# One-hot compares against numbers in spare PSUM columns, the first weighing ahead of the scan, and mask rows, X rows and expert weights at other places

## The chip, the core and the metric

The kernel runs on one core of a Trainium2 chip. The core has five engines that run side by side, each through its own list of instructions in order: TensorE (PE, matrix products; its weight loads are shown as PEld), VectorE (DVE), ScalarE (ACT), GpSimd (POOL) and SyncE (SP, which here only issues transfers). Transfers (DMA) are also issued from ACT and POOL. An engine waits at an instruction until the semaphores that it names have been raised, and everything behind it on that engine waits too. SBUF is the working memory, PSUM the memory into which PE writes, in banks that the kernel names; a bank's tile here has 512 float32 columns on 128 partitions.

The metric is the time of the whole program on the device in microseconds (us).

## The reference

Two blocks in a row. The first is a recurrent cell (mLSTM) over 4 batches, 8 heads, 768 positions, head width 40:

```python
for t in range(S):
    m_new = np.maximum(f_gate[:, :, t] + m, i_gate[:, :, t])
    f_stab = np.exp(f_gate[:, :, t] + m - m_new)
    i_stab = np.exp(i_gate[:, :, t] - m_new)
    m = m_new
    C = f_stab[..., None, None] * C + i_stab[..., None, None] * np.einsum('bhd,bhe->bhde', vt, kt)
    n = f_stab[..., None] * n + i_stab[..., None] * kt
    y[:, :, t] = sigmoid(o) * (C @ q) / np.maximum(np.abs(n @ q), 1.0)
```

Its output, 3072 rows of 320, goes through the second block, a routed layer of 8 experts; a row's expert is a hash of its token number:

```python
expert_idx = token_ids * np.int64(2654435761) % np.int64(E)
for e in range(E):
    mask = expert_idx == e
    h = np.maximum(x[mask] @ w1[e], 0.0)      # 320 -> 1024
    out[mask] = h @ w2[e]                     # 1024 -> 320
```

## The kernel before

**The cell** is computed in 24 steps: step `s` is one batch (`s % 4`) and one block of 128 positions (`s // 4`), all 8 heads. Within a block the recurrence becomes products. For one step:

- PE turns k and q (`turn`, a product with the identity, L396), and a copy brings them to SBUF (`kT`, `qT`, L401, mostly on ACT);
- `scores` (L460): PE multiplies kT and qT into two PSUM banks, `sp0` and `sp1`;
- `decays` (L417 to L429): PE multiplies mask rows (`Rs`) with end rows (`L`, `Lz`) into the banks `ab`, and ACT takes the exponent into `w` (L423);
- `weigh` (L476): DVE multiplies `sp` into `w`, half by half; this frees `sp0` and `sp1` for the next step's scores;
- `apart` (L486, L488): ACT and POOL copy values into `vd`; `k_weights` (L440, `kw`) and the state's updates (`decayed` L500, L522) run on POOL;
- `state` (L512): PE's products for the next state, copied out by ACT (L516, L520); they are written into the bank in which q of step `s + 2` was turned, so they wait until that `qT` is copied;
- `attend` (L533): PE's products of `w` with the values, and of `qs` (L431) with the state, into the banks `xh0` and `xh1` in turn. They use 328 of the 512 columns;
- `divided` (L551 to L560): DVE divides and gates the result (gate: ACT, L449).

The loop over the steps is written out by hand (`for s in range(NT)`, L873), and each engine's order is the order of the code (a manual schedule). Iteration `s` turns k and q of step `s + 2`, scores and weighs step `s + 1`, and attends step `s`. Loads of k, q, v and o run through SP some steps ahead, 160 KB each.

**The gates.** The first block of positions has a short scan of its own (L789, group `g0`). A long scan over all positions (L838, 2.16 us in the profile) gives `m_sb`; from it four blocks are copied to other partitions (`m1`, L906), and group `g1` makes sums (L312 to L314), then three rows `A`, `X` and `e`, each split into bfloat16 parts (`split`, L318 and L319; `rows`, L323). `keep_a` and `keep_e` (L272, L275) store these rows in DRAM from ACT's queue, and `load_a` and `load_e` (L253, L260, L263) bring them back through SP into `Rs`, `L` and `Lz` in another layout; step 4 is the first that uses them. `Rs` also has a constant part, the mask, in its last 64 partitions, written for batch 0 and copied to batches 1 to 3 (L837, L856).

**The routing** runs in pieces between the steps (`pieces`, `products`). In steps 8 to 19 `route_hot` (L717) compares a slot's column and row with the numbers 0 to 127 (`iota_f`, float32 in SBUF): `oh_c` (L720, 94 elements) and `oh_r` (L728, 256 elements), both on DVE; ACT and POOL scale `oh_c` (L724, L725). PE adds them up to a table of indices every third step (L736).

**The passage into the experts.** After the last step the rows `x` are stored to DRAM, gathered by expert through POOL (`gather`, L111; `fetch`, L1188), stored by slot (`x_slots`), and loaded in blocks of 32 (`blocks`, L1205, twelve transfers `xb`), which DVE turns (L1215). Expert 0 takes another way: its rows are turned by PE, the last 32 of them in `turn_rest` (L1220) by way of a tile `remT`. PE fills the time with expert 0's first two tiles. The weights of expert 1 are asked for (`load_weights(1)`, L1235) ahead of the first gathers. Experts 1 to 7 follow one after another, each layer by seven half products in place of eight (L1065, L1073, L1149).

Of the kernel before, what the change touches and what calls it, by code (L numbers as in the profile page):

```python
# [9 lines left out]
F32 = mybir.dt.float32  # L10
# [5 lines left out]
ALU = mybir.AluOpType  # L16
PSUM = bass.MemoryType.PSUM

P = 128
NEG = -1e30  # L20
# [3 lines left out]
def kernel(  # L24
# [24 lines left out]
    nc = tc.nc  # L49
# [145 lines left out]
    with tc.tile_pool(name="gates", bufs=1) as gp, \  # L195
# [202 lines left out]
        def turned_out(s, what, copy=nc.scalar.copy):  # L398
            d = st[s]
            d[what + "T"] = wk.tile([P, PR, P], F32, name=what + "T", bufs=3)  # L400
            copy(d[what + "T"][:], d["tp"][:])  # L401
# [313 lines left out]
        oh_c = gp.tile([P, TH, 3, NC], BF16, name="oh_c")  # L715

        def route_hot(i):  # L717
            half = TH // 3
            ts, th = slice(i * half, (i + 1) * half), slice(i % 3 * half, (i % 3 + 1) * half)
            nc.vector.tensor_tensor(  # L720
                oh_c[:, th, 0], iota_f[:, :NC].unsqueeze(1).to_broadcast([P, half, NC]),
                rc[:, 1, ts].unsqueeze(2).to_broadcast([P, half, NC]), op=ALU.is_equal,
            )
            nc.scalar.activation(oh_c[:, th, 1], oh_c[:, th, 0], AF.Copy, scale=pcol[:, 0:1])  # L724
            nc.gpsimd.tensor_tensor(  # L725
                oh_c[:, th, 2], oh_c[:, th, 0], thi[:, ts].unsqueeze(2).to_broadcast([P, half, NC]), op=ALU.mult,
            )
            nc.vector.tensor_tensor(  # L728
                oh_r[:, th], iota_f[:].unsqueeze(1).to_broadcast([P, half, P]),
                rc[:, 0, ts].unsqueeze(2).to_broadcast([P, half, P]), op=ALU.is_equal,  # L730
            )
# [65 lines left out]
        direct_a(2, nc.sync)  # L797
        nc.gpsimd.memset(Ls[0][:32].rearrange("p b t -> p (b t)").bitcast(F32), 0.0)
        ends_rows(Ls[0])
        load(2, "q")  # L800
# [15 lines left out]
        load(3, "v")  # L816
        load(5, "q")
        g0.ends()
        g0.split("e")
        g0.rows("e", nc.scalar.copy)  # L820
        turned_out(0, "k")
        turned_in(0, "q", "tr")
        turned_out(0, "q", nc.vector.tensor_copy)
        turned_in(1, "k", 0)
        kt = st[1].pop("tp")
# [10 lines left out]
        g0.weights(kwT0)  # L836
        nc.vector.tensor_copy(Rs[HB:, 1], R[HB:])  # L837
        nc.vector.tensor_tensor_scan(m_sb[:, 1:], f_sb[:], i_sb[:], NEG, op0=ALU.add, op1=ALU.max)  # L838
        st[1]["tp"] = kt
        turned_out(1, "k")  # L840
        st[1]["tp"] = qt
        turned_out(1, "q")
        pads(ks[2], qs[2])
        for t in vs[:2]:
            nc.gpsimd.memset(t[:, :, D:], 2.0)
        nc.gpsimd.memset(vds[0][:], 0.0)
        k_weights(0)
# [7 lines left out]
        weigh(0)  # L855
        nc.vector.tensor_copy(Rs[HB:, 2:B], R[HB:].unsqueeze(1).to_broadcast([P - HB, B - 2, H, P]))  # L856

# [15 lines left out]
        for s in range(NT):  # L873
# [20 lines left out]
            if s == 1:  # L894
                g1.rows("e", nc.scalar.copy)
                keep_e(0, g1.zt, nc.scalar)
                load(KV, "k")
            if s == 7:
                nc.scalar.activation(g2.t["X"][:, 0], g2.t["A"][:, 0], AF.Exp)
# [4 lines left out]
            if s == 0:  # L904
                for j in range(NB - 2):
                    nc.scalar.copy(m1[j * BH : (j + 1) * BH], m_sb[:, (j + 1) * P : (j + 2) * P + 1])  # L906
                g1.sums(False)
                g1.split("A")
            if s == 3:
                g1.weights(kwT1)  # L910
            if s + 1 < NT:
                k_weights(s + 1)
            if s == 0:
                nc.gpsimd.memset(vds[1][:], 0.0)
                for t in vs[2:]:
                    nc.gpsimd.memset(t[:, :, D:], 2.0)
                pads(ks[4], qs[4])
            if s + 1 < B:
                nc.gpsimd.memset(Cs[s + 1][1][:], 0.0)
            if s == 1:  # L920
                pads(ks[5], qs[5])
                ends_rows(Ls[1])
                nc.gpsimd.tensor_copy(Lx[:], one[:, 1].to_broadcast([P, HB]))
                load_e(1)
                load(KV - 2, "v")
                load(KV, "q")
                load(KV - 2, "o")
            for piece in pieces.get(s, []):
# [3 lines left out]
            if s + 1 < NT:  # L932
                scores(s + 1)
                decays(s + 1)
            state(s)
            if s == 0:
                nc.scalar.activation(g1.t["X"][:, 0], g1.t["A"][:, 0], AF.Exp)
                g1.rows("A", nc.scalar.copy)
# [8 lines left out]
            gate(s)  # L947
            if s == 0:
                g1.rows("X", nc.scalar.copy)
                keep_a(0, g1.zt, nc.scalar)  # L950
                load_a(B, 2 * B)
                load(3, "o")
            if s == 2:
# [45 lines left out]

    def turn(xg, dst, on_act):  # L1000

# [5 lines left out]
        if on_act:  # L1007
            nc.scalar.copy(dst, tp[:])
        else:
            nc.vector.tensor_copy(dst, tp[:])  # L1010

# [171 lines left out]
    with tc.manual_schedule():  # L1183
# [36 lines left out]
        def turn_rest():  # L1220
            remT = xp.tile([P, DB, P], F32, name="remT", bufs=1)
            turn(xr0, remT[:], True)
            nc.gpsimd.tensor_copy(xT0[:, :, NM:], remT[:, :, :RM])

# [9 lines left out]

        load_weights(1)  # L1235
        fetch(0)
        fetch(1)
        blocks(1)
        h = h0
# [89 lines left out]
```

## Time and profile before

| | us |
|---|---|
| median of 3 runs | 355.13 (354.95 to 355.22) |
| the profiled execution's own time | 349.56 |
| its span, first to last instruction | 347.7 |
| PE busy in it | 330.7 (95%) |
| DVE busy | 234.6 (67%) |
| POOL busy | 208.5 (60%) |
| ACT busy | 131.9 (38%) |

All times of single instructions below come from the one profiled execution. A line of a timeline reads: start, length, engine, line of the code, operation, tile written and tiles read, sizes, count, and in brackets how long the engine had been idle before and what released it. "x2" on a line means that two instructions in a row were put together. A matmul's end is modelled, so a busy PE is not PE at its peak. The chain of work that ended last is followed back from the last instruction, at each step to what released it. In a wait's line stand who waited, for whom, the total in us, how often, and the longest.

### The profile page before, as it was taken

The page shows a single profiled execution, that of the slowest core. Times are in us where ns is not written, and L with a number is a line of the kernel's source. Part 1 is how long each engine was busy: PE and PEld are TensorE (multiplying, and loading weights), DVE is VectorE, ACT ScalarE, POOL GpSimd, SP SyncE. Part 2 cuts the span into 40 slices and gives each one's busy share as a digit, 9 for nine tenths or more (in the row PEclk, how much of TensorE's full clock was granted, in tenths as well). Part 3 has the DMA queues.
Part 4 walks back from the last instruction along what each step waited for, and adds up shares of the span by engine and source line. Part 5 has one row for each costly group of instructions (what it writes and reads, how often), then busy time and mean ns, then how long its engine had stood idle before and what let it go on. Part 6 is the DMA issues. An engine that isn't in the chain of part 4 may idle for free.

```text
span 347.7 us, 10265 instructions
## 1 busy us (share of the span) xinstructions
PE 330.7 (95%) x4059; PEld 292.5 (84%) x4059; DVE 234.6 (67%) x526; ACT 131.9 (38%) x343; POOL 208.5 (60%) x324
## 2 busy tenths in 40 slices
PE   8879997899999899899999999999999999999994
PEld 8668987898999676578899899879989889899892
DVE  6986999999998771137676696734685775764710
ACT  4757666677777431021511411411421501511510
POOL 7783786798885314624925956933954946627613
PEclk9978999999999999999999999999999999999998
DMA  6879898999799989666959658677378478001001
GB/s 127 170 144 183 146 185 150 184 191 201 155 203 261 248 290 309 194 131 149 326 140 272 221 98 266 209 177 254 119 162 277 116 169 251 2 18 41 1 20 41
DMA packets 161960, 59.12 MB, mean 170 GB/s; under 512 B 140372, under 2 KB 157392, under 8 KB 161880
## 3 DMA queue, kind: packets, MB, share of 16 engines
q1 hardware_dynamic: 156678, 47.47, 58.4%
q0 software_dynamic: 3168, 10.49, 9.0%
q10 hardware_dynamic: 2064, 0.48, 0.6%
q8 instruction: 33, 0.54, 0.6%
q14 instruction: 17, 0.14, 0.1%
HBM read 46.25 MB, written 12.33 MB: 168 GB/s over the span
## 4 chain that ended last, share of the span: by engine, by line
PE 75%; DVE 12%; POOL 4%; issue 3%; DMA 3%; ACT 1%; another core or an unknown queue 1%; POOLq 0%; DVEq 0%
PE mh L1065 20%; PE mh L1149 15%; PE mh L1116 10%; PE mh L1073 6%; PE xh L533 6%; PE tr L396 5%; PE sp L460 4%; DVE w L476 2%; DVE oh_c L720 2%; DMA x_rows<-x 1%; PE mh L159 1%; DVE qs L431 1%; POOL xg L111 1%; PE mh L1229 1%; PE ab L419 1%
## 5 line engine op out<-in xcount | busy, mean ns | idle before, releaser
L991 POOL DMA_INDIRECT out_dram<-zo,s_idx x26 | 26.7, 1027 | 67.7 <-issue 41.1
L1116 PE MATMUL mh<-w2t,h 128*128 128x320 f32 x160 | 45.1, 433 | 0.5 <-DVE h L166 0.5
L1116 PEld LDWEIGHTS mh<-w2t,h 128*128 128x128 f32 x160 | 30.0, 190 | 11.8 <-DVE h L166 1.0
L1051 DVE TENSOR_TENSOR h<-u,mh 128x416 f32<-128x416 f32 (+1 forms) x56 | 25.4, 476 | 16.5 <-PE mh L1073 8.6
L111 POOL DMA_INDIRECT xg<-x_rows,g_idx x24 | 23.5, 977 | 15.0 <-issue 6.4
L1065 PE MATMUL mh<-tx,sw 128*128 128x208 f32 x168 | 31.9, 339 | 0.0
L1065 PEld LDWEIGHTS mh<-tx,sw 128*128 128x128 f32 x168 | 29.7, 190 | 0.1
L1051 DVE TENSOR_TENSOR u<-m,mh 128x416 f32<-128x416 f32 x28 | 16.5, 588 | 18.8 <-PE mh L1065 14.9
L1149 PE MATMUL mh<-tw,sh 128*128 128x160 f32 x168 | 27.4, 299 | 0.0
L533 PE MATMUL xh<-v,w 128*64 128x41 f32 x384 | 26.7, 231 | 0.0
L460 PE MATMUL sp<-qT,kT 64*64 64x64 f32 (+1 forms) x960 | 24.5, 238 | 2.3 <-DVE w L476 2.0
L460 PEld LDWEIGHTS sp<-qT,kT 64*64 64x64 f32 x960 | 20.5, 137 | 7.2 <-issue 3.7
L476 DVE TENSOR_TENSOR w<-sp,w 128x384 f32<-128x384 f32 x48 | 24.3, 546 | 2.4 <-ACT w L423 2.3
L533 PEld LDWEIGHTS xh<-v,w 128*64 128x64 f32 x384 | 25.2, 141 | 0.0
L1149 PEld LDWEIGHTS mh<-tw,sh 128*128 128x128 f32 x168 | 24.3, 190 | 0.0
L423 ACT ACTIVATE w<-ab 128x384 f32<-128x384 f32 x48 | 21.0, 482 | 7.5 <-PE ab L422 4.8
L1065 PE MATMUL mh<-xT,w1t 128*128 128x208 f32 x112 | 23.1, 339 | 0.0
L522 POOL TENSOR_TENSOR C<-C,add 40x164 f32<-40x164 f32 x32 | 16.2, 505 | 9.2 <-ACT dec L495 6.8
L1073 PE MATMUL mh<-xT,w1c 64*128 64x208 f32 x224 | 21.6, 342 | 0.0
L1079 ACT COPY m<-mh 128x416 f32<-128x416 f32 x14 | 7.1, 506 | 37.2 <-PE mh L1065 34.2
L1149 PE MATMUL mh<-w2t,h 128*128 128x160 f32 x112 | 21.0, 300 | 0.0
L987 ACT COPY zo<-mh 128x320 f32<-128x320 f32 x12 | 5.1, 427 | 41.9 <-PE mh L1116 26.7
(276 smaller groups left out, 859.7 us busy)
## 6 DMA issues: line engine op xcount, KB each, us to landing
w2t<-in_moe_w_dram SPq DMA_DIRECT2D x7, 1280.0 KB
w1t<-in_moe_w_dram SPq DMA_DIRECT2D x7, 1024.0 KB
xb<-x_slots SPq DMA_DIRECT2D x84, 52.0 KB
k<-in_k_dram SPq DMA_DIRECT2D x24, 160.0 KB
v<-in_v_dram SPq DMA_DIRECT2D x24, 160.0 KB
og<-in_o_gate_dram SPq DMA_DIRECT2D x24, 160.0 KB
q<-in_q_dram SPq DMA_DIRECT2D x23, 160.0 KB
x_slots<-xg SPq DMA_DIRECT2D x7, 480.0 KB
```

Source lines behind the costliest of these rows:

```text
L111: nc.gpsimd.indirect_dma_start(out=xg, out_offset=None, in_=x_d[:rows, :], in_offset=bass.IndirectOffsetOnAxis(ap=idx, axis=0),)
L396: nc.tensor.transpose(tp[:, j, :], d[what][:, 2 * j : 2 * j + 2, :].rearrange("p h d -> p (h d)"), ident[:])
L423: nc.scalar.activation(w[:, hf], ab, AF.Exp)
L460: nc.tensor.matmul(sp[hf][o * HB : (o + 1) * HB, m, bs], lhsT=kT[r, 2 * m + j, i], rhs=qT[r, 2 * m + j, ts], start=True, stop=True,)
L476: nc.vector.tensor_tensor(d["w"][:, hf], d["sp"][hf], d["w"][:, hf], op=ALU.mult)
L533: nc.tensor.matmul(xh[half[i], hs], lhsT=lhsT, rhs=rhs, start=first[i], stop=last, skip_group_check=True)
L991: ins = nc.gpsimd.indirect_dma_start(out=out[:, :], out_offset=bass.IndirectOffsetOnAxis(ap=idx, axis=0), in_=zo[:], in_offset=None, bound ...
L1051: nc.vector.tensor_tensor(o, a, b, op=ALU.add)
L1065: nc.tensor.matmul(pair(bank[n])[:, a], lhsT=lhsT(g + a), rhs=rhs, start=first and a == 0, stop=True, skip_group_check=True,)
L1073: nc.tensor.matmul(pair(bank[n])[:, a], lhsT=w1c[k, g + a, :], rhs=xT[k, 2, r], start=False, stop=True, skip_group_check=True,)
L1116: nc.tensor.matmul(zp, lhsT=h[:, fb, j * P : (j + 1) * P], rhs=w[2][:, fb, :], start=(fb == 0), stop=(fb == FB - 1),)
L1149: nc.tensor.matmul(bank[n], lhsT=lhsT(f), rhs=rhs(f), start=first and f == 0, stop=f == FB // 2 - 1, skip_group_check=True,)
```

## The change

- **Compares.** Two ACT copies, in iterations 4 and 5, write `iota_f` into columns 384 to 511 of the banks `xh1` and `xh0`, which `attend` leaves unused. `route_hot` reads the numbers from there; in each iteration it takes the bank that `divided` has just read, not the one that PE is writing.
- **Start.** The first weighing comes ahead of the long scan on DVE. The mask copies L837 and L856 become one, ahead of most of the start's DVE work. Two of the four copies to `m1` go from ACT to POOL, and they and the sums of `g1` come after step 1's `kw`. Some POOL memsets come earlier.
- **Rows.** Making and storing the rows `X` and `e` of `g1` goes from iterations 0 and 1 to behind the state products of iteration 1. The loads of these rows, and of q 6 and o 4, come behind the gate of iteration 1; o 3 is asked for before the loop, k 6 and v 4 ahead of the rows.
- **Passage.** `turn_rest` copies 32 columns straight to `xT0`, by ACT, without `remT` and POOL. `load_weights(1)` comes after the first two fetches.

```diff
+        numbers = [t[:, 3 * P :] for t in xhs]
+
         def route_hot(i):
             half = TH // 3
+            iota = numbers[(i + 1) % 2]
...
-                oh_c[:, th, 0], iota_f[:, :NC].unsqueeze(1).to_broadcast([P, half, NC]),
+                oh_c[:, th, 0], iota[:, :NC].unsqueeze(1).to_broadcast([P, half, NC]),
...
-                oh_r[:, th], iota_f[:].unsqueeze(1).to_broadcast([P, half, P]),
+                oh_r[:, th], iota[:].unsqueeze(1).to_broadcast([P, half, P]),
...
         nc.gpsimd.memset(Ls[0][:32].rearrange("p b t -> p (b t)").bitcast(F32), 0.0)
+        pads(ks[2], qs[2])
+        for t in vs[:2]:
+            nc.gpsimd.memset(t[:, :, D:], 2.0)
+        nc.gpsimd.memset(vds[0][:], 0.0)
         ends_rows(Ls[0])
...
         load(5, "q")
+        load(3, "o")
...
         turned_out(0, "q", nc.vector.tensor_copy)
+        nc.vector.tensor_copy(Rs[HB:, 1:B], R[HB:].unsqueeze(1).to_broadcast([P - HB, B - 1, H, P]))
...
         g0.weights(kwT0)
-        nc.vector.tensor_copy(Rs[HB:, 1], R[HB:])
-        nc.vector.tensor_tensor_scan(m_sb[:, 1:], f_sb[:], i_sb[:], NEG, op0=ALU.add, op1=ALU.max)
...
-        pads(ks[2], qs[2])
-        for t in vs[:2]:
-            nc.gpsimd.memset(t[:, :, D:], 2.0)
-        nc.gpsimd.memset(vds[0][:], 0.0)
...
         weigh(0)
-        nc.vector.tensor_copy(Rs[HB:, 2:B], R[HB:].unsqueeze(1).to_broadcast([P - HB, B - 2, H, P]))
+        nc.vector.tensor_tensor_scan(m_sb[:, 1:], f_sb[:], i_sb[:], NEG, op0=ALU.add, op1=ALU.max)
...
             if s == 1:
-                g1.rows("e", nc.scalar.copy)
-                keep_e(0, g1.zt, nc.scalar)
                 load(KV, "k")
+                load(KV - 2, "v")
...
             if s == 0:
-                for j in range(NB - 2):
+                for j in range(2):
                     nc.scalar.copy(m1[j * BH : (j + 1) * BH], m_sb[:, (j + 1) * P : (j + 2) * P + 1])
-                g1.sums(False)
-                g1.split("A")
...
                 k_weights(s + 1)
             if s == 0:
+                for j in range(2, NB - 2):
+                    nc.gpsimd.tensor_copy(m1[j * BH : (j + 1) * BH], m_sb[:, (j + 1) * P : (j + 2) * P + 1])
+                g1.sums(False)
+                g1.split("A")
...
-                load_e(1)
-                load(KV - 2, "v")
-                load(KV, "q")
-                load(KV - 2, "o")
...
             state(s)
+            if s == 1:
+                g1.rows("X", nc.scalar.copy)
+                keep_a(0, g1.zt, nc.scalar)
+                g1.rows("e", nc.scalar.copy)
+                keep_e(0, g1.zt, nc.scalar)
...
             gate(s)
-            if s == 0:
-                g1.rows("X", nc.scalar.copy)
-                keep_a(0, g1.zt, nc.scalar)
+            if s in (4, 5):
+                nc.scalar.copy(numbers[(s - 1) % 2], iota_f[:])
+            if s == 1:
                 load_a(B, 2 * B)
-                load(3, "o")
+                load_e(1)
+                load(KV, "q")
+                load(KV - 2, "o")
...
-    def turn(xg, dst, on_act):
+    def turn(xg, dst, on_act, n=P):
...
-            nc.scalar.copy(dst, tp[:])
+            nc.scalar.copy(dst, tp[:, :, :n])
...
-            remT = xp.tile([P, DB, P], F32, name="remT", bufs=1)
-            turn(xr0, remT[:], True)
-            nc.gpsimd.tensor_copy(xT0[:, :, NM:], remT[:, :, :RM])
+            turn(xr0, xT0[:, :, NM:], True, RM)
...
-        load_weights(1)
         fetch(0)
         fetch(1)
+        load_weights(1)
         blocks(1)
```

More of the change, by code (lines that the diff above doesn't have):

```diff
@@ L1007, in turn @@
         if on_act:
-            nc.scalar.copy(dst, tp[:])
+            nc.scalar.copy(dst, tp[:, :, :n])
         else:
-            nc.vector.tensor_copy(dst, tp[:])
+            nc.vector.tensor_copy(dst, tp[:, :, :n])
     def bank(i):
```

## The prediction

> **What bounds the kernel now.** I read the page first, then the chain of work that ended last in order of time, then single engines' timelines at the places where the chain leaves PE. Columns of the chain: start, length, engine, tile, line.
>
> ```profile
> span 347.7 us, 10265 instructions
> PE 75%; DVE 12%; POOL 4%; issue 3%; DMA 3%; ACT 1%; another core or an unknown queue 1%; POOLq 0%; DVEq 0%
> ```
>
> ```profile
> 9.91 0.42 DVE Rs L837
> 10.36 2.16 DVE m_sb L838
> 12.53 0.91 DVE w L476 x2
> 13.47 2.30 DVE Rs L856
> ...
> 22.88 1.93 PE xh L533 x21
> 24.81 1.90 PE tr L396 x8
> 26.71 1.43 PE sp L460 x32
> ...
> 33.85 0.93 PE xh L533 x21
> 35.06 0.87 PE tr L396 x8
> 35.93 0.86 PE sp L460 x32
> ...
> 55.87 1.79 DVE oh_c L720
> ...
> 60.06 0.51 DVE xh L559
> ...
> 61.16 1.73 DVE oh_c L720
> ...
> 65.29 0.51 DVE xh L559
> ...
> 70.11 0.86 PE sp L460 x32
> ...
> 74.46 0.86 PE sp L460 x32
> ...
> 79.98 1.00 DVE oh_c L720
> ```
>
> Three quarters of the chain are PE, and those the change leaves alone. It touches three places where PE is held: the start (10 to 33 us), steps 8 to 10 and 13 (55 to 82 us), and the passage into the experts (126 to 160 us). I call the gains there A, B and C.
>
> **A, the start.**
>
> ```profile
> 10.19 1.00 ACT L423 ACTIVATE w<-ab 128x384 f32<-128x384 f32 x2 [0.27 <-PE ab L422]
> 12.73 1.23 ACT L906 COPY m<-m_sb 32x129 f32<-32x129 f32 x4
> ...
> 19.70 0.41 ACT L323 COPY zt<-X_zt 128x256 bf16<-128x256 bf16 x1 [1.59 <-DVE X_zt L318]
> ...
> 20.56 0.59 ACT L401 COPY kT<-tr 128x512 f32<-128x512 f32 x1 [0.46 <-PE ab L422]
> ...
> 21.52 0.42 ACT L323 COPY zt<-e_zt 128x256 bf16<-128x256 bf16 x1
> ...
> 22.41 0.33 ACT L486 COPY vd<-v 64x164 f32<-64x164 f32 x1 [0.47 <-POOL L L376]
> ```
>
> ```profile
> 21.73 0.78 PE L512 MATMUL tr<-v,kw 128*40 128x41 f32 x16 [1.28 <-issue]
> ```
>
> ```profile
> DVE L L835 <- ACT L L834: 1.9, 1, 1.9
> ```
>
> *DVE.* Today the first weighing starts at 12.53, behind the scan (2.16), though the first half of its exponent was ready at about 10.7 (10.19 and half of 1.00). Behind it stands the mask copy (2.30), and the gate sums start at its end, 15.8. In the new order weighing runs 10.7 to 11.7, the scan to 13.9. Of the four copies of the scan's result (1.23/4 = 0.31 each) two go to POOL, beside the other two; so the sums start at about 14.7, 1.1 earlier. The mask copy goes to the DVE idle of 1.9 ahead of L835: at 0.42 for a third of it, about 1.3, hidden; without that cover it would cost up to 2.3. The POOL memsets that move ahead only exchange places with POOL work that is not yet waited for; POOL's two copies cost at most 0.6 there.
>
> *ACT.* ACT is free at 18.1 (19.70 less the wait of 1.59), but the kT copy starts at 20.56: 2.45 us go to waiting for X, its rows and the issue of their store. From 21.52 to 22.41 another 0.9 goes to the e rows and their store. Both leave, so the vd copy that releases PE's values at 22.88 could end 3.3 earlier. Next late is then PE itself: the decays of step 2 end at 20.45 (21.73 less 1.28 idle), 1.1 earlier by the DVE, 19.35; after half a us of state products the values start at about 19.9 instead of 22.9: **3.0**.
>
> *Clock.*
>
> ```profile
> 22.00:24.00 2.00, 1.63 (x34) 1.51 (x30) 1.54 (x4) 1.56 (x5) 1.71 (x5) 0.50 0.24 66
> ```
>
> In this row (PE, PEld, DVE, ACT, POOL busy, granted clock, DMA share, GB/s) PE ran at half clock. The three blocks from 22.88 took 1.93 + 1.90 + 1.43 = 5.26, the same blocks later 0.93 + 0.87 + 0.86 = 2.66. Without the stall ahead of them I expect full clock: **2.6**. It could be nothing (a rival below).
>
> The fall came behind idle stretches of 1.28 at most. The Trainium skill, "TensorE: Matmul & The Clock Gate", Part 1, has the clock halved after an idle window of about 3.4 us. By that rule a busier PE cannot be gated here and the 2.6 is safe; but by it the clock should not have fallen before either, so the trace disagrees, and I leave room for a gate that also falls in the new order.
>
> *What is paid.* The X and e rows with both stores (about 1.7 of ACT) now stand in step 1, ahead of its gate and of step 2's kT and qT copies, for which PE's state products wait. That costs between 0 and 1.7; I take 0.6, since ACT waits for PE's transposes there. Second, the mask and end rows come back through DRAM later:
>
> ```profile
> SPq L244 <- DMA gate_rows<-zt: 4.7, 1, 4.7
> ```
>
> ```profile
> 27.96 0.36 SPq L263 DMA_DIRECT2D Lz<-gate_ends  x1
> ```
>
> ```profile
> 32.81 0.30 PE L419 MATMUL ab<-Rs,Lz 128*64 128x256 bf16 x1
> ```
>
> Today the store goes out at 20.1, the last load back (Lz) at 27.96, 7.8 later, and step 4's decays use it at 32.81. In the new order the store goes out at about 20.9 (state products copied out at 20.4, X rows 0.4). With the same 7.8, Lz goes out at 28.7, and PE wants it at 32.81 - 5.0 = 27.8; the landing comes on top (below the 4.9 from 27.96 to 32.81). So the bounds are 0 and 5. Against that, SP's 4.7 of waiting for that store falls on fewer loads: o of step 3, k of 6 and v of 4 now go ahead of the rows. I take 0.5, near the lower end. **A = 3.0 + 2.6 - 0.6 - 0.5 = 4.5**.
>
> **B, the compares.**
>
> ```profile
> L720 DVE TENSOR_TENSOR oh_c<-iota_f,rc x12: 364/1050/1874, 55.8 to 106.8; 128x94 bf16<-128x94 f32 x12
> ```
>
> ```profile
> 62.05 0.71 POOL L440 TENSOR_TENSOR kw<-k,kwT 128x320 f32<-128x320 f32 x1
> ```
>
> The same compare of 94 elements takes 0.36 to 1.87 (ns: least, median, most), so most of it is waiting. It ends at 62.9 in step 9 and POOL's kw ends at 62.76: it waits until POOL's row of operations is over. DVE sets the step there, 60.06 to 65.29 = 5.23, against 70.11 to 74.46 = 4.35 where PE sets it. With 0.36 the DVE's step is 5.23 - 1.73 + 0.36 = 3.9, so PE's 4.35 is next: 0.88 in each of the two steps with 1.79 and 1.73, and about 0.4 each in the next step and in that of 79.98 (PE has the table products there). **B = 2.5**, from 0 to 3.
>
> The Trainium skill, "SBUF — State Buffer", section "Who interferes with whom", says that a VectorE instruction with two SBUF inputs contends with a GpSimd one that reads SBUF, and one with a single SBUF input does not. By it the wait is gone and B stands; without it B is 0. No compare with a PSUM operand is in this trace.
>
> The two copies of the numbers into the banks (steps 4 and 5) are 128 elements on ACT, some 0.3 each by the vd copy (0.33 for 164), beside PE; uncovered 0.6.
>
> **C, the passage into the experts.**
>
> ```profile
> 138.94 2.42 PE L1116 MATMUL mh<-w2t,h 128*128 128x320 f32 x8 [0.46 <-DVE h L166]
> ...
> 148.48 1.35 PE L159 MATMUL mh<-xT,w1t 128*128 128x160 f32 x8 [2.15 <-POOL xT L1223]
> ```
>
> ```profile
> 147.62 0.48 ACT L1008 COPY remT<-mh 128x384 f32<-128x384 f32 x1 [5.75 <-PE mh L1116]
> ```
>
> ```profile
> 145.40 0.37 SPq L1196 DMA_DIRECT2D x_slots<-xg  x1
> ```
>
> ```profile
> 157.44 1.47 DVE L1215 STREAM_TRANSPOSE xT<-xb 128x1248 f32<-128x1248 f32 x1
> ```
>
> ```profile
> 132.00:134.00 2.00, 2.00 (x13) 1.52 (x13) 0.00 (x0) 0.04 (x1) 0.00 (x0) 1.00 1.09 355
> ...
> 144.00:146.00 2.00, 2.00 (x11) 1.38 (x9) 0.00 (x0) 0.00 (x0) 1.59 (x2) 1.00 0.60 169
> ```
>
> PE waits 2.15 for the last 32 columns of xT. Today ACT copies 384 columns (147.62) and POOL 96 of them on; the new code copies the 96 at once: PE can start at about 147.9 instead of 148.48, 0.6. Why ACT starts only at 147.62 no row tells; if that goes too, another 1.5. The 0.46 ahead of 138.94 is DVE held by the gather; the gather comes sooner when expert 1's weights no longer load beside the last x store: 0.46. Sum 1.1 to 2.6; I take **C = 1.5**, near the lower end.
>
> What is paid: the weights now go out behind the x_slots store at 145.40. They are 2 x 320 x 1024 x 4 B = 2.62 MB: 7.4 us at 355 GB/s, so they land at 153.2, and expert 1's twelve xb loads queue behind. DVE wants those at 157.44, less what C gains. At 355 GB/s that fits.
>
> **The sum.** 4.5 + 2.5 + 1.5 = 8.5 off the profiled execution's 349.56 (span 347.7 and 1.86 around it): 341.1. The shown runs have a median of 355.13, 5.57 above the profiled one; I carry that over: 355.13 - 8.5 = **346.6**.
>
> **The rivals.**
> - *The start stays cold, or the rows come late.* Short idle stretches still halve the clock, or PE waits at step 4 for Lz: A = 4.5 - 2.6 = 1.9, total 5.9, 349.2. For: the clock fell behind 1.28 of idle; 7.8 us of round trip. Against: PE has less idle in the new order.
> - *The compares still wait* (the change does not do what it says): rc is still read from SBUF beside POOL. B = 0, 349.1. Against: the weighing, with one operand in PSUM, takes 0.91 for two halves (12.53) with POOL at work beside it.
> - *Expert 1's weights come late.* If they share the DMA engines with gathers and stores, xb lands some 4 later than wanted: C = -2.5, total 4.5, 350.6.
> - *Slower.* The same queue at its worst: the weights get only the 169 GB/s of 144 to 146 us (15.5, until 161.3) and the twelve xb loads follow one after another, 4.4 more at the 0.37 that SP needs for an issue: 165.7, 8.3 later than 157.44. Then PE waits 8.3, A and B give 7: 1.3 slower, 356.4. It decides from a landing at 164.4 (below some 185 GB/s). Against: most gathers are over by then.
>
> **How the numbers follow.** Forecast 0.57, cold start or late rows 0.20, compares 0.07, weights late 0.10, slower 0.04, all given back (no change) 0.02. Lower end: A 5.0, B 3.0, C 2.6, 344.5, with 0.5 for the spread of runs 344.0. Upper end: the third rival and 1.2 for parts of two rivals together, 351.8. About 0.2% is what a measurement of this kernel can tell from no change. Faster 0.94, within 0.2% 0.02, slower 0.04.
>
> **What would show it.** Right: first weighing near 10.7; step 1's values near 20 at full clock; no oh_c compare over 0.5; steps 9 to 11 at 4.4 to 4.6; no PE idle ahead of L159. Wrong: a granted clock of 0.5 at 20 to 28 us; PE waiting for ab at step 4; compares still ending with POOL's kw; PE idle at the first products of expert 1 on xb or weights.

## The result, and the profile after

| | before | after |
|---|---|---|
| median of the runs taken side by side | 354.2 us | 357.46 us |
| the profiled execution | 349.56 us (span 347.7) | 357.73 us (span 355.8) |

The changed kernel takes 1.0119 times as long, with a 95% interval of 1.0072 to 1.0167: **1.2% slower**, where 346.6 us and a gain had been forecast. The ratio and its interval are taken from the faster runs of each kernel, those within 1.5% of its fastest, while the medians are of all twenty.

Read stage by stage, the two traces tell where the time went. Their sizes need care: the profiled execution of the kernel before is a quick one, 4.6 us under its median, that of the changed kernel 0.3 over its own. So of the 8.2 between the two some 4 are the change's (1.2%), and the rest is the spread between executions, to which the last experiments come back. First the page of the changed kernel, its span and the shares of the chain that ended last:

```profile
span 355.8 us, 10265 instructions
...
PE 63%; DMA 9%; DVE 8%; POOL 6%; issue 5%; SPq 5%; ACT 2%; POOLq 0%; DVEq 0%; ACTq 0%
```

PE held 75% of the chain before. Now it holds 63%; DMA has gone from 3 to 9, and SP's queue (SPq), which was not there, has 5. So the chain has left the engine that the change relieved. The three places in order:

**The start came true in its order, though not in its size.** DVE's timeline, then PE's, of the changed kernel (start, length, engine, line, operation, out<-in; in brackets the idle time ahead of it and what ended it):

```profile
10.05 1.07 DVE L476 TENSOR_TENSOR w<-sp,w 128x384 f32<-128x384 f32 x2 [0.55 <-ACT w L423]
...
14.29 0.29 DVE L312 TENSOR_TENSOR a_zt<-f,m 128x128 f32<-128x128 f32 x1 [1.51 <-POOL m L915]
```

```profile
19.58 0.26 PE L533 MATMUL xh<-vd,w 128*64 128x82 f32 x1
...
29.73 0.30 PE L419 MATMUL ab<-Rs,Lz 128*64 128x256 bf16 x1 [1.26 <-DMA Lz<-gate_ends]
...
46.26 0.93 PE L460 MATMUL sp<-qT,kT 64*64 64x128 f32 x40
...
51.68 0.93 PE L460 MATMUL sp<-qT,kT 64*64 64x128 f32 x40
...
56.04 0.93 PE L460 MATMUL sp<-qT,kT 64*64 64x128 f32 x40
...
82.65 0.93 PE L460 MATMUL sp<-qT,kT 64*64 64x128 f32 x40
```

The weighing starts at 10.05, the gate sums at 14.29, step 1's values at 19.58 (before: 12.53, 15.8, 22.88). PE does wait for the late Lz row, 1.26.

**The compares came true.** From the scores at 51.68 on, the steps last 4.36. The answer on the tile oh_c (least, median, most, in ns) has no waiting compare left:

```profile
L723 DVE TENSOR_TENSOR oh_c<-xh,rc x12: 247/248/249, 52.6 to 102.5; 128x94 bf16<-128x94 f32 x12
```

The same marks in PE's timeline of the kernel before:

```profile
49.36 0.93 PE L460 MATMUL sp<-qT,kT 64*64 64x128 f32 x40
...
88.25 0.93 PE L460 MATMUL sp<-qT,kT 64*64 64x128 f32 x40
```

So the changed kernel is 3.1 ahead at the scores of step 8, where the compares begin (46.26 against 49.36), and 5.6 ahead at the scores of step 16 (82.65 against 88.25). That lead is then lost, and more than the lead, in two places.

**First loss: the tail of the attention.** The chain of waits of the changed kernel in order of time (start, length, what), only its DMA pieces:

```profile
89.52 3.62 DMA gate_ends<-zt
...
94.42 4.33 DMA v<-in_v_dram
...
106.57 5.81 DMA v<-in_v_dram
...
119.02 6.05 DMA xg<-x_rows,g_idx
```

In the kernel before this stretch of the chain is PE nearly throughout, from 83.96 to 109.70. Now it hangs on transfers: the store of the gate ends, two loads of v, and the gather of expert 0's rows. Four marks show where the lead goes. They are lines of SP's, PE's, POOL's and DVE's timelines, first of the changed kernel:

```profile
89.52 0.44 SPq L275 DMA_DIRECT2D gate_ends<-zt  x1
...
114.03 1.38 PE L460 MATMUL sp<-qT,kT 64*64 64x128 f32 x40
...
117.66 1.06 POOL L111 DMA_INDIRECT xg<-x_rows,g_idx  x1 [9.36 <-DVE qs L431]
...
125.09 0.20 DVE L970 COPY xg<-xg 128x64 f32<-128x64 f32 x1 [2.67 <-DMA xg<-x_rows,g_idx]
```

and of the kernel before (where DVE's copy does not wait):

```profile
89.37 0.38 SPq L275 DMA_DIRECT2D gate_ends<-zt  x1
...
120.21 1.39 PE L460 MATMUL sp<-qT,kT 64*64 64x128 f32 x40
...
115.54 1.06 POOL L111 DMA_INDIRECT xg<-x_rows,g_idx  x1 [2.88 <-DVE den L552]
```

PE is 5.6 ahead at step 16, but SP, which issues the loads one behind the other, stands at the same place at the same time (89.52 and 89.37). So its second store of the first ten steps' results goes out no earlier either (108.41, before 107.53), and the gather, which needs those rows, goes out 2.1 later. The wait for a v load costs PE 1.3 of its lead at step 20; at the scores of step 23, its last, it is still 6.2 ahead (114.03 against 120.21). Nearly all is lost behind that: POOL stands 9.36 at the gather, with the copy of `vd` for which PE waits behind it in its list, and DVE waits for the gathered rows. The table by stretches of ten us shows what PE does meanwhile (PE, PEld, DVE, ACT, POOL busy, granted clock, DMA share, GB/s):

```profile
110.00:120.00 10.00, 6.31 (x160) 5.39 (x160) 7.61 (x20) 4.73 (x14) 2.04 (x3) 0.94 0.90 237
120.00:130.00 10.00, 7.61 (x75) 6.61 (x76) 2.93 (x14) 1.33 (x3) 2.23 (x5) 0.55 0.82 275
```

It idles in part from 110 on, and from 120 its clock is down to 0.55. The lead has become a lag of 2.3 at the first product of expert 0 (L159: 128.97, before 126.64, both below).

**Second loss: the passage.** PE's timeline of the changed kernel, then of the kernel before:

```profile
128.97 1.99 PE L159 MATMUL mh<-xT,w1t 128*128 128x256 f32 x8
...
163.34 1.76 PE L1072 MATMUL mh<-xT,w1t 128*128 128x208 f32 x4 [4.86 <-DVE xT L1222]
165.91 4.36 PE L1072 MATMUL mh<-tx,sw 128*128 128x208 f32 x12 [0.81 <-DVE tx L1034]
```

```profile
126.64 1.99 PE L159 MATMUL mh<-xT,w1t 128*128 128x256 f32 x8
...
159.12 0.87 PE L1065 MATMUL mh<-xT,w1t 128*128 128x208 f32 x4
159.82 2.34 PE L1065 MATMUL mh<-tx,sw 128*128 128x208 f32 x12
```

Expert 1's products start 4.2 later, wait within their first group, and run at a lowered clock (0.66 granted from 160 to 170 us): the group of 12 takes 4.36 in place of 2.34. They wait for DVE's transpose, DVE for xb, and xb for SP. SP's timeline, changed kernel first, kernel before second:

```profile
143.35 0.37 SPq L1203 DMA_DIRECT2D x_slots<-xg  x1
143.82 0.43 SPq L98 DMA_DIRECT2D w1t<-in_moe_w_dram  x1
...
147.25 12.61 SPq L1218 DMA_DIRECT2D xb<-x_slots  x12
```

```profile
148.67 6.08 SPq L1211 DMA_DIRECT2D xb<-x_slots  x12
```

The x_slots store is 2.05 earlier than before (145.40), yet the twelve loads behind the weights take 12.61 to issue where they took 6.08, and end 5.1 later. All that follows is shifted by this wait and the lowered clock: 8.1 at the end of the span (355.8 less 347.7).

### The profile page after: what moved, and what is told of

It reads as the page before. It is cut to its first block, busy times and chain, and to the rows that moved or that the text cites. A ratio compares the mean times of both kernels' runs of the same rounds, so it can differ in the third digit from the quotient of the medians.

```text
span 355.8 us, 10265 instructions
## 1 busy us (share of the span) xinstructions
PE 331.9 (93%) x4059; PEld 293.9 (83%) x4059; DVE 229.4 (64%) x525; ACT 131.7 (37%) x343; POOL 206.5 (58%) x325
## 4 chain that ended last, share of the span: by engine, by line
PE 63%; DMA 9%; DVE 8%; POOL 6%; issue 5%; SPq 5%; ACT 2%; POOLq 0%; DVEq 0%; ACTq 0%
PE mh L1072 20%; PE mh L1156 15%; PE mh L1123 8%; PE mh L1080 6%; PE xh L533 3%; SPq L1218 3%; PE tr L396 3%; DMA xg<-x_rows,g_idx 3%; DMA v<-in_v_dram 3%; PE sp L460 2%; DVE w L476 2%; PE mh L1234 1%; DVE qs L431 1%; DMA gate_ends<-zt 1%; PE ab L419 1%
## 5 line engine op out<-in xcount | busy, mean ns | idle before, releaser
L1072 PE MATMUL mh<-tx,sw 128*128 128x208 f32 x168 | 33.9, 354 | 0.8 <-DVE tx L1034 0.8
L1072 PEld LDWEIGHTS mh<-tx,sw 128*128 128x128 f32 x168 | 31.5, 200 | 1.5 <-DVE tx L1034 1.4
L1072 PE MATMUL mh<-xT,w1t 128*128 128x208 f32 x112 | 24.0, 348 | 4.9 <-DVE xT L1222 4.9
L533 PE MATMUL xh<-v,w 128*64 128x41 f32 x384 | 27.5, 235 | 0.0
L533 PEld LDWEIGHTS xh<-v,w 128*64 128x64 f32 x384 | 26.1, 145 | 0.0
L1072 PEld LDWEIGHTS mh<-xT,w1t 128*128 128x128 f32 x112 | 20.3, 195 | 5.4 <-DVE xT L1222 5.4
L533 PE MATMUL xh<-vd,w 128*64 128x82 f32 x192 | 20.8, 251 | 3.7 <-issue 3.7
L460 PE MATMUL sp<-qT,kT 64*64 64x64 f32 (+1 forms) x960 | 23.6, 233 | 0.5 <-DVE w L476 0.3
```

The lines of the kernel that those rows point to most:

```text
L460: nc.tensor.matmul(sp[hf][o * HB : (o + 1) * HB, m, bs], lhsT=kT[r, 2 * m + j, i], rhs=qT[r, 2 * m + j, ts], start=True, stop=True,)
L533: nc.tensor.matmul(xh[half[i], hs], lhsT=lhsT, rhs=rhs, start=first[i], stop=last, skip_group_check=True)
L1072: nc.tensor.matmul(pair(bank[n])[:, a], lhsT=lhsT(g + a), rhs=rhs, start=first and a == 0, stop=True, skip_group_check=True,)
```

## The experiments

Two theories had to be told from their rivals. **P** (the passage): the weights of expert 1, put ahead of xb on SP's queue, cost 4 to 6 us. **S** (supply): the tail of the attention is set by the row loads, and what start and compares gain is waited away there. For S spoke rows that the prediction had not looked at, the same table by stretches for the kernel before:

```profile
60.00:70.00 10.00, 9.13 (x236) 8.19 (x234) 9.49 (x22) 6.93 (x21) 7.25 (x16) 1.00 1.00 180
70.00:80.00 10.00, 10.00 (x279) 9.14 (x280) 9.45 (x24) 7.42 (x21) 9.15 (x18) 1.00 1.02 199
80.00:90.00 10.00, 9.52 (x258) 8.60 (x254) 9.50 (x24) 6.69 (x19) 8.88 (x18) 1.00 1.07 206
```

The last but one number is the DMA share: the engines were already full from 60 to 90 us, at some 200 GB/s. Ratios are to the kernel before in runs on the same chip; that kernel's median differed between the groups of runs (351.8 to 355.3), so only ratios are compared across groups.

### Each part alone

**The weights put back ahead, in the changed kernel:**

```diff
+        load_weights(1)
         fetch(0)
         fetch(1)
-        load_weights(1)
```

> The changed kernel with one thing put back: the weights of expert 1 are loaded ahead of the first fetches again, as in the kernel before. Theory P (the passage: behind the fetches the weights' 2.62 MB stand ahead of expert 1's twelve xb loads on the same queue, and xb lands about 4 us late): 4 to 6 us less than the changed kernel, ratio to the kernel before 0.995 to 1.001, and DVE's transpose of xb starts within 3 of the end of the attention plus 30, as before, with no idle PE at the first products of expert 1. Rival (the loss comes from the attention alone, and the weights only fill time that was lost already): ratio stays near 1.012.

Measured: 0.9991 (0.9956 to 1.0026). The changed kernel's 1.0119 less this is 1.3%, 4.5 us. PE's wait at expert 1 fell from 4.86 to 1.39, in PE's timeline of this run:

```profile
162.10 0.97 PE L1072 MATMUL mh<-xT,w1t 128*128 128x208 f32 x4 [1.39 <-DVE xT L1222]
```

P holds, though not all idle time went. It also says that the rest of the change, for which some 8 of the 8.5 us had been forecast, brings nothing that can be measured (1.6 us at most by the interval).

**The same move alone, in the kernel before:**

```diff
-        load_weights(1)
         fetch(0)
         fetch(1)
+        load_weights(1)
```

> The kernel before with that one move alone: the weights of expert 1 behind the two fetches. Theory P: 4 to 6 us slower, ratio 1.011 to 1.017, with PE idle 3 or more at the first products of expert 1. Rival (the prediction's sum: the weights fit, and the gather comes 0.46 sooner): ratio 0.998 to 1.001.

Measured: 1.0193 (1.0146 to 1.0241), 6.8 us slower, a little over what P gave. SP's and PE's timelines show the same two marks:

```profile
148.73 14.29 SPq L1211 DMA_DIRECT2D xb<-x_slots  x12
```

```profile
166.82 1.76 PE L1065 MATMUL mh<-xT,w1t 128*128 128x208 f32 x4 [5.54 <-DVE xT L1215]
```

**The compares alone, in the kernel before** (weights, start and rest rows as before):

```diff
+            iota = numbers[(i + 1) % 2]
...
-                oh_c[:, th, 0], iota_f[:, :NC]...
+                oh_c[:, th, 0], iota[:, :NC]...
...
+            if s in (4, 5):
+                nc.scalar.copy(numbers[(s - 1) % 2], iota_f[:])
```

> The kernel before with the compares' numbers in the output banks alone. The prediction's B: 2.5 us less, ratio 0.993. Theory S (the tail of the attention is set by the row loads, whose DMA engines are busy 0.87 to 1.07 of the time from 30 to 120 us, so what PE gains in steps 8 to 13 is waited away later): the steps 9 to 11 shrink to 4.3 to 4.6 and scores of step 14 start 2 earlier, but step 23 starts at most 0.7 earlier and the ratio is 0.997 to 1.001. Third theory (the copies into the banks or the new reads cost): ratio above 1.002.

Measured: 1.0016 (0.9984 to 1.0049): nothing. Yet the compares themselves do all that was forecast, as the tile's row shows:

```profile
L723 DVE TENSOR_TENSOR oh_c<-xh,rc x12: 248/250/250, 54.9 to 104.8; 128x94 bf16<-128x94 f32 x12
```

At the end of the attention DVE's copies of the gathered rows wait, here 2.76 and then 2.55 more (DVE's timeline), and the gather itself only goes out at 119.87 (POOL's):

```profile
124.35 0.20 DVE L968 COPY xg<-xg 128x64 f32<-128x64 f32 x1 [2.76 <-DMA xg<-x_rows,g_idx]
```

```profile
119.87 1.06 POOL L111 DMA_INDIRECT xg<-x_rows,g_idx  x1 [9.33 <-DVE qs L431]
```

**The start alone, in the kernel before** (all hunks of the change but those of the compares, the weights and the rest rows):

> The kernel before with the start of the changed kernel alone (first weighing ahead of the scan, mask rows and X rows at their new places); compares, expert 1's weights and the copy of the rest rows as before. The prediction's A: 4.5 us less, ratio 0.987. Theory S: step 8 starts some 3 earlier, but the end of the attention is at most 1 earlier, ratio 0.997 to 1.002. Third theory (the new order harms the tail by itself): ratio above 1.004.

Measured: 0.9967 (0.9941 to 0.9993), 1.2 us faster, a quarter of the 4.5. S's limit of 1 us was about right.

### Is it the loads?

Fewer packets, the same bytes, read from other rows of DRAM, once in the kernel before and once in e1:

```diff
-                eng.dma_start(og[s][:], rows_of(o_gate, s))
+                eng.dma_start(og[s].rearrange("p h d -> p (h d)"), moe_w2[s % 8, :P, :])
```

> The kernel before, with the 24 loads of o reading whole rows of the second weights (128 packets of 1280 B) in place of o's rows (640 packets of 256 B): the same bytes, a fifth of the packets; o's values are left out of the result. Theory S (the DMA engines, busy with 256 B packets, set the tail of the attention; PE sets it only up to step 16): DMA share of 60 to 110 us falls from about 1.0 to about 0.8, SP's last v load goes out 4 or more earlier, and since PE of the kernel before was hardly later than the loads, the gain is 1 to 4 us: ratio 0.989 to 0.997. Rival (PE and its helpers set the tail): DMA share falls, ratio 0.998 to 1.002.

> The changed kernel with expert 1's weights ahead of the fetches again, and the same wide loads of o (o's values left out of the result). Theory S: with the loads out of the way the gains of the start and of the compares reach the end of the attention: no wait for v over 1, the gather of the first expert rows goes out 4 or more earlier than in e1, and it beats the run with wide loads of o in the kernel before by 4 to 6 us (ratio to the kernel before 0.972 to 0.984). Rival G (not the loads but the landing of the gather alone holds the tail): v waits go, but the time is that of e1 (ratio 0.996 to 1.002).

Measured: 0.9843 (0.9791 to 0.9895) for e5 and 0.9725 (0.9669 to 0.9780) for e6, medians 348.27 and 343.23 of the same group of runs. With the loads relieved, start, compares and rest rows together bring 5.0 us; with the loads as they are they brought nothing (e1). That is S's main prediction, and the rival that only the gather's landing counts falls as it was put, though the gather came earlier too. e5 gained a little more than expected: its last v load goes out at 102.22 in place of 110.60, though its DMA share did not fall evenly (0.82, 1.01 and 0.69 in the three stretches from 60 to 90 us). In e6 the gather goes out at 108.58, 9.6 ahead of e1. The first products of expert 0 in e5, then of expert 0 and expert 1 in e6, with no wait for the transpose (PE's timelines):

```profile
123.08 1.99 PE L159 MATMUL mh<-xT,w1t 128*128 128x256 f32 x8
```

```profile
119.81 1.99 PE L159 MATMUL mh<-xT,w1t 128*128 128x256 f32 x8
...
152.13 0.87 PE L1072 MATMUL mh<-xT,w1t 128*128 128x208 f32 x4
```

**Packets or bytes?** In e1, o's loads cut to the first half of each row:

```diff
-                eng.dma_start(og[s][:], rows_of(o_gate, s))
+                w = D if s < 6 else D // 2
+                eng.dma_start(og[s][:, :, :w], rows_of(o_gate, s)[:, :, :w])
```

(o's six buffers are fixed tiles here, so that the half not loaded holds an earlier step's values.)

> e1 with the loads of o from step 6 on reading the first half of each row only (640 packets of 128 B in place of 256 B; the second half of o's values is left from an earlier step, so the result leaves them out). If packets set the pace of the row loads: no gain on e1, ratio 0.996 to 1.003. If bytes set it: an eighth of the row loads' bytes less, and most of the gain of e6: ratio 0.975 to 0.988.

Measured: a median of 351.2 with runs from 341.38 to 355.27, beside 355.26 for the kernel before; the runs spread too far for an interval. Inconclusive in time. In the one trace of it the scores keep their pace of 4.35 to 4.7 up to step 22, where e1 lost 1.6 at step 20, so there half the bytes relieved the loads too, which speaks against packets alone; the gather still went out at 114.54 and DVE waited 4.9 for it. What the pace depends on, packets, bytes or SP's place for a next transfer, stays open.

### Where in the tail?

**The early transposes of the gathered rows behind the last step, in e1:**

```diff
-            if s == NT - 2:
-                for j in range(2):
-                    nc.vector.tensor_copy(xg0[:, j, Dm:], xg0[:, j, 2 * P : Dm])
-                early_turn(0)
...
         store(NT - 1, nc.gpsimd)
+        for j in range(2):
+            nc.vector.tensor_copy(xg0[:, j, Dm:], xg0[:, j, 2 * P : Dm])
+            early_turn(j)
```

(and `early_turn(1)` of step 23 likewise)

> e1 with the copies and transposes of the gathered rows (which stand ahead of DVE's division of step 22 and of PE's work of step 23) behind the last step. Loads and stores as in e1. If the wait for the gather only holds DVE and PE in order (rival G): the division of step 22 starts near 119.5 in place of 126.9, that of step 23 near 122.5 in place of 130.4, the first products of expert 0 start about 2.5 earlier, ratio 0.990 to 0.995. If the attention's own loads hold it: ratio as e1, 0.997 to 1.002.

Measured: 0.9996 (0.9962 to 1.0030). A miss: the divisions did move ahead (step 22 at 121.44 in place of 126.89, step 23 at 123.06 in place of 130.43), and expert 0's first products with them (126.55 in place of 130.32), but the second gather then took 6.31 where it took 3.65 in the kernel before, and expert 1's products start at 163.15, no earlier than in e1 (162.10). Freeing DVE and PE alone moves the wait on.

**SP's two stores of the first ten steps' results five steps ahead, in e1:**

```diff
-            if s in (18, 19):
-                store_first((s - 18) * LS // 2, (s - 17) * LS // 2)
+            if s in (13, 14):
+                store_first((s - 13) * LS // 2, (s - 12) * LS // 2)
```

> e1 with SP's two stores of the first ten steps' results in steps 13 and 14 in place of 18 and 19: the same transfers, at a place where the row loads still have a lead of some 10 us. Theory S with the gather as its last link (the gather waits for the second store, which waits in SP's queue behind row loads): the gather goes out near 110 in place of 118, DVE does not wait for it, the attention ends 4 to 7 earlier than in e1, ratio 0.980 to 0.990. Rival (the DMA engines have no room anywhere: the same bytes only move, and rows of k and v are now late): waits for k or v grow by 3 or more, ratio 0.997 to 1.005.

Measured: 0.9872 (0.9819 to 0.9924). The gather goes out 6.7 earlier than in e1, at 111.50 (POOL's timeline of e8, below), and expert 0's first products start at 123.34 in place of 130.32. That the gather now waits 0.61 and no longer 9.69 shows that it was the store that it had waited for, whatever engine its row names. The row loads are later for it, as the rival had it, but by less than the 3 that it named: the scores of step 20 come 7.2 after those of step 19, in e1 5.9. The chain has one wait for v:

```profile
111.50 1.06 POOL L111 DMA_INDIRECT xg<-x_rows,g_idx  x1 [0.61 <-DVE ta L760]
```

```profile
96.07 3.73 DMA v<-in_v_dram
```

So both S and its rival have a part: a transfer at a better place frees the gather, but the row loads pay for it.

### Do the gains pass when the transfers stand better?

Four kernels with the stores of e8 and the last row loads a step later; with neither part, with both, with the start, with the compares (the last three with the rest rows copied at once):

```diff
-            if s == B * (NB - 2):
-                fetch_rows(s + B)
+            if s == B * (NB - 2) + 1:
+                fetch_rows(s + B - 1)
```

> The kernel before with its transfers moved only: SP's two stores of the first ten steps' results in steps 13 and 14 in place of 18 and 19, and the loads of the last four steps' rows from DRAM one step later than their store in place of right behind it (SP stood 3.6 for that store's landing in e1). Theory S: the gather goes out near 111, nothing waits for it; PE sets the rest, so a few us at most: ratio 0.985 to 0.996. Rival (in the kernel before PE alone sets the tail): 0.998 to 1.002.

> The changed kernel with expert 1's weights ahead of the fetches and the same two moves of transfers, so e8 with the row loads a step later. Theory S: the wait of 3.7 for a v load after it shrinks to under 2, step 20 starts near 100.5 in place of 102.6, the first products of expert 0 near 121 in place of 123.3: ratio 0.975 to 0.985, and 4 to 6 us less than e9 (the gains of start and compares pass). Rival D (the DMA engines themselves, busy 1.0 from 60 to 120 us, hold the tail wherever the transfers stand): the wait only moves to another load; ratio as e8, 0.985 to 0.990, and under 2 us less than e9.

> e10 with the compares as in the kernel before (their numbers in SBUF): the start alone, with relief. Theory S: some 2 slower than e10, 3 to 4 faster than e9. Rival D: within 1 us of e10.

> e9 with the compares on numbers in the output banks (and the rest rows copied at once, as in e10): the compares alone, with relief. Theory S: about 2 faster than e9, 3 slower than e10. Rival D: within 1 us of both.

| kernel | median | ratio to before |
|---|---|---|
| e9, the kernel before with relief | 349.97 | 0.9882 (0.9806 to 0.9958) |
| e10, start and compares | 348.18 | 0.9849 (0.9785 to 0.9913) |
| e11, start | 346.43 | 0.9776 (0.9706 to 0.9845) |
| e12, compares | 348.19 | 0.9883 (0.9816 to 0.9951) |

The relief alone is worth 1.2%. On top of it the two parts together bring 1.8 us by the medians, not 4 to 6, and the intervals overlap. But in the one trace of e9 there was little to pass on: PE ran its start at full clock and its first compares hardly waited (both below), so the scores of step 16 start at 84.19, only 1.5 behind e10's 82.74. In e11 and e12 they start at 85.00 and 84.86. Expert 0's first products start at 124.95, 125.38, 123.23 and 124.82 in e9 to e12: whoever led at step 16 does not lead there. That is what rival D says, that the row loads hold the tail wherever the other transfers stand; how much of a larger lead would pass, these four runs do not show. Nor did e10's marks come: expert 0's first products start at 125.38, not near 121, and its chain has two waits for v in place of e8's one:

```profile
88.71 5.31 DMA v<-in_v_dram
...
95.77 5.18 DMA v<-in_v_dram
```

e11 is the fastest of the four, 2.2% under the kernel before; that it beats e10 is not settled by these intervals.

### Was the profile of before typical?

The kernel before twice more and the changed kernel once more, each for its trace.

> The kernel before once more, for its trace. If the typical execution is paced in its tail like e2's: DVE waits 2 or more for the gathered rows, the division of step 22 starts near 127 in place of 124.7, the first products of expert 0 near 130 in place of 126.6, time 353 to 356. If the first profile is typical: 124.7 and 126.6 again, time 349 to 351.

> The kernel before a third time, with the same two outcomes as in the run before it.

> The changed kernel once more, for its trace: the first products of expert 0 near 129 to 131, those of expert 1 5 or more later than in the kernel before, on xb.

Measured: 351.83, 353.59 and 357.67. PE's timelines, e14, e15 and e16 in this order:

```profile
161.42 0.87 PE L1065 MATMUL mh<-xT,w1t 128*128 128x208 f32 x4
```

```profile
163.17 0.87 PE L1065 MATMUL mh<-xT,w1t 128*128 128x208 f32 x4
```

```profile
125.80 1.99 PE L159 MATMUL mh<-xT,w1t 128*128 128x256 f32 x8
...
163.59 1.75 PE L1072 MATMUL mh<-xT,w1t 128*128 128x208 f32 x4 [8.07 <-DVE xT L1222]
```

Three profiles of the same kernel reach expert 1 at 159.12, 161.42 and 163.17: the one that the prediction was worked out from is the fastest of them. In e15 DVE waits for the gather (1.97), in the first two it does not. And e16 is the clearest case for P: its attention ends 3.2 earlier than in the first profile of the changed kernel (125.80 against 128.97), and expert 1 starts at the same moment (163.59 against 163.34). What was gained ahead of the passage did not reach the end.

## Why the prediction was wrong

- **A, the start (4.5): right in its order, about half in its size, and it did not reach the end.** Weighing was forecast for 10.7 and came at 10.05, the sums 14.7 and 14.29, step 1's values 19.9 and 19.58. The late Lz row, taken at 0.5, shows as a wait of 1.26 at step 4. At the scores of step 8 the two traces are 3.1 apart. But the kernel before is not always that late there: all ten traces with the new start have these scores at 45.7 to 46.3, the eight with the old one at 47.3 to 49.4, on the average 2.2 later, and the prediction's profile is the latest of the eight. Alone the start was worth 1.2 us of the total (e4).
- **The clock (2.6 of A): mis-sized.** In the first profile of the changed kernel no stretch of the start is at 0.5, as forecast; in the kernel before the row of 22 to 24 us was at 0.50. That this came true is luck in part, for the fall comes and goes between executions of the same code. The changed kernel has it in e16, behind an idle time of 1.70:

```profile
16.00:18.00 2.00, 1.77 (x8) 1.37 (x8) 1.97 (x5) 0.90 (x2) 1.84 (x5) 0.50 1.14 200
```

And e9, whose start is that of the kernel before, has 1.00 in all rows from 16 to 28 us, with the same idle 1.28 ahead of its state products. Worked out from the rows of two us, the half clock lasted some 6.8 us in the profile from which 2.6 was taken, 3.4 in e15 and nothing in e9. So the rival of the cold start was not answered by a busier PE; what sets the moment of the fall stays open. The changed kernel's clock also falls elsewhere, to 0.55 from 120 to 130 us, and at expert 1's first products, behind idle times of 3.72 (to 120.38) and 4.86 (to 163.34). By the Trainium skill, "TensorE: Matmul & The Clock Gate", Part 1, an idle window of about 3.4 us halves the clock. The fall at expert 1 agrees with it. That in the tail does not, since the clock was at 0.50 from 119 us on, 2.3 us into the idle time; nor does that at 22 us in the kernel before, where 1.44 (ahead of 13.12) and 1.28 are PE's longest idle times from 8 us on.
- **B, the compares (2.5): right step by step, and worth nothing at the end.** 0.25 for every compare and steps of 4.36; another 2.5 between step 8 and step 16 (3.1 to 5.6). e3 has all of it and no time. The rule that was weighed there, of the Trainium skill, "SBUF — State Buffer", section "Who interferes with whom", is borne out: with one operand in PSUM the compare's 364 to 1874 ns became 247 to 249, with POOL as busy as before (206.5 us in place of 208.5).
- **C, the passage (1.5): the hop left, the gain did not.** In the changed kernel and in e1 PE has no idle ahead of L159 there, as forecast; then it waits for xb instead. In e6 and e8, where all comes earlier, 2.15 and 1.81 of idle stand there again, now for ACT's copy of the 96 columns, which starts late as it did before the change. What holds ACT there stays open, as it was in the prediction.
- **The step that failed first, in "The sum": "4.5 + 2.5 + 1.5 = 8.5 off the profiled execution's 349.56".** Local gains were added up as if PE set every stage behind them. The chain of waits did say PE for 75%, but the DMA share of 1.00 to 1.07 from 60 to 90 us was in the same trace, and no rival asked what is late next in the tail of the attention. It was the row loads, SP's stores behind them, and the gather behind those (e3, e5, e6, e8). PE's gain does not move SP's queue, and what waits for that queue stays where it was: PE's lead of 5.6 at step 16 was a lag of 2.3 at expert 0.
- **The step that failed second, in "What is paid" under C: "At 355 GB/s that fits".** Two errors. The weights took until about 156, not 153.2 (an estimate from the rates of all transfers: 309 GB/s from 154 to 156 us, 100 in the next two). And the xb loads, "queue behind", were given no time of their own: they took 6.08 to issue with nothing ahead of them and 12.61 behind the weights, so DVE's transpose came at 161.81 where 157.44 less the gain was wanted. The third rival had this as "some 4 later"; the slower rival had the order of things, weights and then the twelve loads one after another, with a chance of 0.04, though with its own sizes: weights at 169 GB/s and a landing at 165.7, where the xb loads landed at 161.5. That its 356.4 is near the measured time is luck, since it has A and B bring 7 and PE wait 8.3. It named 164.4 as the point from which it decides only because it counted on the 7 of A and B. Without them any lateness is a loss: 6.8 us alone (e2).
- **The base.** 5.57 was carried over from the profiled execution to the median. e14 and e15 say that this gap is not a constant: in these two it is where the gather and xb land late, so in the stages that the change made worse.

## What to carry to other kernels

Before gains are summed, look at the DMA share of the stages *behind* the gain: where it stands near 1.0, as here, an engine that gets ahead may only eat the lead of its loads; compare where the issuing queue stands before and after, and let the sum stop at the transfer that comes next. A bulk load put ahead of small ones on the same queue is not paid with its bytes alone: count the time that the small ones need by themselves and add it (6.08 here, and with the weights ahead 12.61 to 14.29). And take the profile of the kernel before more than once where its runs spread by more than the gain that is forecast.

## What the runs showed of the hardware

The DMA engines were full at very different rates. In the kernel before, with rows of 256 B, a share of 1.00 went with 180 GB/s; in the changed kernel, with the weights under way, 1.09 went with 389 (the table by stretches of two us):

```profile
152.00:154.00 2.00, 2.00 (x18) 1.76 (x17) 0.66 (x3) 0.30 (x1) 0.00 (x0) 1.00 1.09 389
```

That is over twice the rate. The Trainium skill, "DMA: Bandwidth & Descriptors", section "Why small descriptors are slow (HBM only)", names two costs of a small descriptor and gives a figure for one of them, 27% of overhead at 256 B; the two rows, which hold other transfers as well, differ by more. Whole rows of 1280 B for one load in four were worth 1.6% of the kernel (e5); that halving the bytes also kept the pace of the scores in the trace of e13 speaks against packets alone.

How long a compare with two SBUF operands waits is not fixed by the code. In e9, with the numbers in SBUF as in the kernel before, the first three took 0.25, 0.46 and 0.60 us where that kernel's took 1.87, 1.81 and 1.02, and its scores of steps 9, 10 and 11 followed each other by 4.36 with no change to the compares:

```profile
L720 DVE TENSOR_TENSOR oh_c<-iota_f,rc x12: 248/354/1084, 53.6 to 106.3; 128x94 bf16<-128x94 f32 x12
```

There POOL was at other operations when the compares ran; why, no run here shows. In the other seven traces with the numbers in SBUF the longest is 1.86 or more.
